# Casts of step 1's folds one step later where they stand at step 2 of a chunk

## The chip, the cores and the metric

The kernel runs on one core of a Trainium2 chip. The metric is the device time of one execution in microseconds (us); lower is better. Five engines of the core run side by side, each working through its own list of instructions in order: TensorE (PE in the profile, with its weight loads as PEld), VectorE (DVE), ScalarE (ACT), GpSimd (POOL) and SyncE (SP, which here only issues DMAs). They wait for each other by semaphores.

## The reference

The input `x` is 8 x 3136 x 256 in fp32. It goes through a two-dimensional Fourier transform of which the real part is kept, and then through one block of layer norm, two matrix products with a ReLU between them, and a residual sum:

```python
X = np.fft.fft(X, axis=1); X = np.fft.fft(X, axis=2); x = X.real
mu = np.mean(x, axis=-1, keepdims=True)
var = np.mean((x - mu) ** 2, axis=-1, keepdims=True)
xn = (x - mu) / np.sqrt(var + 1e-06) * g_ln
ch = np.maximum(xn @ w_ch1, 0.0) @ w_ch2          # 256 -> 1024 -> 256
return x + ch
```

## The kernel before

**Two halves that overlap.** The Fourier transform along the 3136 rows is done per batch b (0 to 7) in two steps with matmuls by tables (64 x 49). Step 1 works on 7 pieces of a batch; its results go to a scratch in memory and come back in another layout (`relayout`). Step 2 (line 309) turns them into columns of a *chunk*: 49 chunks of 256 tokens (the last is larger), each with its values (`ck`), their rounded part (`ckh`) and the rest (`ckl`). The norm and both products, here called the MoE part, run over the chunks. Products are made in three passes of rounded and rest operands (`hi`, `lo`), because one pass of the fast fp32r format is not exact enough.

**The main loop.** Line `for s in range(6, last)` counts steps; chunk c has the steps 8c to 8c+7, one per 128 of the 1024 inner columns. Below, "step 2 of its chunk" means s % 8 == 2. A step issues, in this order:

- `moe1_b(s-1)`: `h_hi` of the step before (ReLU and rounding, ACT, L368), and the rest `h_lo` (DVE, L369, which reads `h` and `h_hi`).
- `moe1_a(s)`: 6 matmuls into the PSUM tile `ab` (L354; two buffers, so the matmuls of step s need that the ones of step s-2 have been read), a copy of one half (`asb`, ACT, L359), and the sum and difference `h` (DVE, L360 and L361, which read `asb` and `ab`).
- what the table `late` holds for the step; `moe2(s-3)`: 12 matmuls (L404) of `h_hi`, `h_lo` with the second weights; and then what the table `after` holds for the step.

Nothing but these two tables, written out in the lines 606 to 669, and the order within a step set where an instruction stands on its engine. PE's list runs up to a step ahead of ACT's and DVE's.

**1/std.** For each chunk c the variance is ready in step 1 of the next chunk, where ACT takes the root (`std`, L460). In step 2 of that next chunk (`inverse_std` in `late` at 8c+10; for the chunks 0 and 1 one step later) four small DVE instructions on 128 x 2 values make 1/std: L467 (one input), then L468, L469 and L471, each with two inputs in SBUF. In the steps 3 and 4 `finish` (L477, L479) scales the product by it and adds the residual; these read PSUM and SBUF. `residual` (L428) is the last dimension's transform, at step 5, into the PSUM tiles that `finish` has freed.

**Step 1's folds.** For batches 1 to 7 a piece at step d (for batch 1 at d+1; list `steps1`) is prepared on POOL and ACT: `fold_zw` (two POOL sums, L207 and L208, listed at d-7), `fold_eo` (two POOL sums into `f`, L213 and L214, at d-6), `fold_hi` (the cast `fh` of `f`, ACT, L219, at d-4), `fold_lo` (the rest `fl`, POOL, L225, which reads `f` and `fh`, at d-3), and then `step1` (three matmuls, L262) and `store1`. All are in `after`, at the end of their step. `f`, `fh` and `fl` have two buffers each. POOL works in order and does little else, so it does `fl` of a piece as soon as ACT has cast it, and then goes straight on to the sums of the pieces that follow, long before the steps at which these are listed.

Before the change the 49 casts stand at the end of the steps 12, 15, 18, 21, 23, 26, 29 (batch 1), 34, 43, 44, 50, 58, 67, 74 (batch 2), and so on. 22 of them stand at step 2 of a chunk, 16 at step 3.

Of the kernel before, what the change touches and what calls it, by code (L numbers as in the profile page):

```python
# [146 lines left out]
def tile_kernel(ctx: ExitStack, tc: tile.TileContext, x, g_ln, w1, w2, tu, tab, tz, ty, tw, out):  # L147
# [460 lines left out]
    def add(s, fn, *args):  # L608

        after.setdefault(s, []).append((fn, args))  # L610
# [25 lines left out]
    for b in range(1, NB):  # L636
        need = 8 * (b * REG // CW) - 3
        at = steps1[b]
        ends_at = need - (58 if b > 1 else 30)
        add(need - 62 if b > 1 else ends_at - 7, ends, b)  # L640
        add(ends_at, step1_ends, b)
        for i, d in enumerate(at):
            d0, d = d, d - (b == 1)
            add(d - 7, fold_zw, b, i, nc.gpsimd)
            if b + 1 < NB:
                add(d - 5, load_x, b + 1, i)
            add(d - 6, fold_eo, b, i)
            add(d - 4, fold_hi, b, i)
            add(d - 3, fold_lo, b, i)
            add(d0, step1, b, i)  # L650
            add(d0, store1, b, i)
        add(at[-1] + 2, relayout, b)
# [201 lines left out]
```

## Time and profile before

| | |
|---|---|
| time, median of 3 runs | 1012.02 us (1011.04 to 1012.07) |
| the profiled execution | 1010.0 us, of which the span shown is 1008.2 us |
| granted TensorE clock in it | 0.999 |
| PE busy | 993.7 us, 99% of the span |
| DVE busy | 833.4 us, 83% |
| ACT busy | 534.6 us, 53% |
| POOL busy | 240.2 us, 24% |
| casts `fh` (ACT, L219) | 49 of 627 ns in the mean |
| rests `fl` (POOL, L225) | 49 of 1307 ns |
| 1/std, L468, L469, L471 (DVE) | 48 each of 394, 338 and 305 ns |

A row of a timeline has the start in us from the beginning of the span, the duration in us, the engine, line and operation, the tile written and the tiles read, shapes, and in brackets the idle time of the engine before the instruction with what ended it. A matmul's end is modelled: matmuls of 256 columns start 0.113 to 0.118 us apart and are shown 0.28 us long, so PE counts as busy in gaps of less than 0.16 us, and an idle time shown is that much too short. A row of the view by stretches has the stretch, its length, and for each engine the busy us and the number of instructions. A few matmul records are missing.

### The profile page before, as it was taken

To read this page: it belongs to the slowest core of one execution; us is meant where nothing else is said; L and a number is where in the kernel's file an instruction comes from. 1 tells how busy PE (TensorE), PEld (TensorE's weight loads), DVE (VectorE), ACT (ScalarE), POOL (GpSimd) and SP (SyncE) were. 2 spreads that over 40 slices of the span, in tenths; PEclk is the share of its full clock that TensorE was granted. 3 is DMA by queue.
4 is the path that set the end of the run, shared out by engine and by line. 5 is a ranking of instruction groups with operands and counts; after the bars stand their busy time and mean duration, and the time that the engine had idled before them with its cause. 6 is when DMAs were issued, how large, how long until landed. Compare 5 with 4: busy or idle time off the path is not lost.

```text
span 1008.2 us, 21760 instructions
## 1 busy us (share of the span) xinstructions
PE 993.7 (99%) x8289; PEld 969.7 (96%) x8289; DVE 833.4 (83%) x2190; ACT 534.6 (53%) x1416; POOL 240.2 (24%) x278
## 2 busy tenths in 40 slices
PE   9999999999999999999999999999999999999998
PEld 6799999999999999999999999999999999999998
DVE  6788887888888888887888887888888878887887
ACT  3655555554654555555555555554655555454553
POOL 1146433124212232312341125123322200000000
PEclk9999999999999999999999999999999999999999
DMA  9933352214221243121521242211311113100101
GB/s 344 262 145 125 107 161 81 79 58 136 86 93 54 75 141 100 55 74 62 170 74 64 84 129 93 90 58 64 116 43 43 53 43 96 43 23 22 43 22 43
DMA packets 41528, 92.10 MB, mean 91 GB/s; under 512 B 4176, under 2 KB 18704, under 8 KB 40528
## 3 DMA queue, kind: packets, MB, share of 16 engines
q1 hardware_dynamic: 40016, 88.87, 26.7%
q8 instruction: 66, 1.08, 0.5%
q0 software_dynamic: 320, 1.05, 0.3%
q10 hardware_dynamic: 1088, 0.79, 0.2%
q14 instruction: 38, 0.31, 0.1%
HBM read 50.32 MB, written 40.37 MB: 90 GB/s over the span
## 4 chain that ended last, share of the span: by engine, by line
PE 80%; DVE 13%; ACT 3%; DMA 2%; issue 2%; SPq 0%; ACTq 0%; DVEq 0%
PE acc L404 43%; PE ab L354 22%; PE ps L309 5%; DVE h_lo L369 4%; PE psy L428 4%; PE ps L262 3%; DVE h L361 2%; DVE h L360 2%; ACT h_hi L368 2%; DVE st L450 1%; DVE ve L468 1%; DVE ve L469 1%; DMA scratch<-s 1%; ACT s L265 1%; PE ps L255 1%
## 5 line engine op out<-in xcount | busy, mean ns | idle before, releaser
L404 PE MATMUL acc<-w_hi,h_lo 128*128 128x256 f32 x1568 | 435.7, 278 | 0.1
L404 PE MATMUL acc<-w_lo,h_hi 128*128 128x256 f32 x1568 | 435.5, 278 | 0.0
L404 PE MATMUL acc<-w_hi,h_hi 128*128 128x256 f32 x1568 | 435.5, 278 | 0.0
L368 ACT ACTIVATE h_hi<-h 128x512 fp32r<-128x512 f32 x392 | 249.7, 637 | 322.2 <-DVE h L361 322.1
L369 DVE SCALAR_TENSOR_TENSOR h_lo<-h,h_hi 128x512 fp32r<-128x512 f32 x392 | 287.5, 733 | 141.8 <-ACT h_hi L368 140.7
L404 PEld LDWEIGHTS acc<-w_hi,h_hi 128*128 128x128 f32 x1568 | 295.6, 189 | 0.0
L404 PEld LDWEIGHTS acc<-w_lo,h_hi 128*128 128x128 f32 x1568 | 295.1, 188 | 0.0
L404 PEld LDWEIGHTS acc<-w_hi,h_lo 128*128 128x128 f32 x1568 | 294.6, 188 | 0.4 <-DVE h_lo L369 0.3
L354 PE MATMUL ab<-ckl,w_hi 128*128 128x256 f32 x768 | 220.4, 287 | 6.5 <-DVE h L361 6.4
L354 PE MATMUL ab<-ckh,w_lo 128*128 128x256 f32 x768 | 213.9, 278 | 0.5 <-ACT ckh L330 0.4
L354 PE MATMUL ab<-ckh,w_hi 128*128 128x256 f32 x768 | 213.4, 278 | 0.0
L225 POOL TENSOR_TENSOR fl<-f,fh 128x512 fp32r<-128x512 f32 x49 | 64.1, 1307 | 527.1 <-ACT fh L219 478.4
L360 DVE TENSOR_TENSOR h<-asb,ab 128x256 f32<-128x256 f32 x384 | 158.3, 412 | 1.6 <-ACT asb L359 1.5
L361 DVE TENSOR_TENSOR h<-asb,ab 128x256 f32<-128x256 f32 x384 | 158.3, 412 | 0.0
L354 PEld LDWEIGHTS ab<-ckl,w_hi 128*128 128x128 f32 x768 | 144.3, 188 | 12.5 <-issue 7.6
L354 PEld LDWEIGHTS ab<-ckh,w_lo 128*128 128x128 f32 x768 | 144.7, 188 | 3.1 <-ACT ckh L330 0.5
L354 PEld LDWEIGHTS ab<-ckh,w_hi 128*128 128x128 f32 x768 | 144.8, 189 | 0.0
L359 ACT COPY asb<-ab 128x256 f32<-128x256 f32 x384 | 138.2, 360 | 10.8 <-PE ab L354 9.2
L265 ACT COPY s<-ps 128x508 f32<-128x508 f32 x56 | 32.8, 585 | 64.3 <-PE ps L262 50.5
L309 PE MATMUL ps<-tab_s,s 112*128 112x98 f32 (+1 forms) x512 | 65.5, 273 | 0.9 <-DMA s<-scratch 0.9
L309 PEld LDWEIGHTS ps<-tab_s,s 112*128 112x128 f32 x512 | 61.8, 191 | 1.4 <-PE pw L678 1.4
L330 ACT CAST ckh<-ps 128x392 fp32r<-128x392 f32 (+49 forms) x112 | 39.8, 356 | 29.5 <-PE ps L309 29.3
(108 smaller groups left out, 981.8 us busy)
## 6 DMA issues: line engine op xcount, KB each, us to landing
xs<-x SPq DMA_DIRECT2D x56, 512.0 KB, 4.1
out<-o SPq DMA_DIRECT2D x96, 256.0 KB, 2.0
scratch<-s SPq DMA_DIRECT2D x49, 256.0 KB, 2.3
s<-scratch SPq DMA_DIRECT2D x7, 1792.0 KB, 9.8
w1p_all<-w SPq DMA_DIRECT2D x8, 512.0 KB, 8.1
scratch<-s POOLq DMA_DIRECT2D x4, 256.0 KB, 6.1
s<-scratch SPq DMA_DIRECT2D x2, 448.0 KB, 5.6
s<-scratch SPq DMA_DIRECT2D x1, 896.0 KB, 12.0
```

The source lines that it names most:

```text
L225: nc.gpsimd.tensor_tensor(out=lo, in0=f, in1=hi.bitcast(F32), op=ALU.subtract)
L265: nc.scalar.copy(s[:, :, :, :127], ps[:, :, :, :127])
L309: nc.tensor.matmul(ps[:, h, k0 - base:k1 - base], s2[b][:KP, g, 128 * h:128 * h + 128], tab_s[:, h, k0:k1], start=(h == 0 and g == 2 * j), ...
L330: nc.scalar.copy(hi, src)
L354: nc.tensor.matmul(pt, wt[wi][:, j, fs], ch[xi][:, j, :w], start=(n == 0), stop=(n == 2))
L359: nc.scalar.copy(asb[:, :w], pa)
L360: nc.vector.tensor_tensor(out=h[:, :w], in0=asb[:, :w], in1=pb, op=ALU.add)
L361: nc.vector.tensor_tensor(out=h[:, w:], in0=asb[:, :m], in1=pb[:, :m], op=ALU.subtract)
L368: nc.scalar.activation(h_hi, h, AF.Relu)
L369: nc.vector.scalar_tensor_tensor(out=h_lo, in0=h, scalar=0.0, in1=h_hi.bitcast(F32), op0=ALU.max, op1=ALU.subtract)
L404: nc.tensor.matmul(acc[c, i][:, side], hs[xi][:, h0:h0 + 128], ws[wi][:, f], start=(f == 0 and side == 0 and n == 0), stop=(f == 7 and n = ...
L428: nc.tensor.matmul(ps[:, j, :129 + j], ck[:, j], ty_s[:, j, :129 + j], start=(j == 0), stop=True, skip_group_check=True)
```

## The change

Two lines of `tile_kernel` become three. `d` is the step that the piece's preparation is counted from. A piece with `d % 8 == 6` had its cast at d-4, which is step 2 of a chunk, and its rest at d-3; both go one step further back. All other pieces stay as they are.

```diff
         for i, d in enumerate(at):
             d0, d = d, d - (b == 1)
             add(d - 7, fold_zw, b, i, nc.gpsimd)
             if b + 1 < NB:
                 add(d - 5, load_x, b + 1, i)
             add(d - 6, fold_eo, b, i)
-            add(d - 4, fold_hi, b, i)
-            add(d - 3, fold_lo, b, i)
+            cast = (d - 4, d - 3)[d % 8 == 6]
+            add(cast, fold_hi, b, i)
+            add(cast + 1, fold_lo, b, i)
             add(d0, step1, b, i)
             add(d0, store1, b, i)
```

22 casts move from step 2 to step 3: those at 18, 26, 34, 50, 58, 74, 82, 106, 114, 130, 154, 162, 178, 194, 210, 218, 242, 258, 266, 290, 298 and 314. The lists of PE, DVE and SP keep their order. No instruction is added or removed.

**ACT, the steps 106 and 107** (batch 3, piece 4; in the names, the number of the step or of batch and piece comes first, the last number is the buffer's own). Before:

```order
L368 ACTIVATE h_hi105_4440<-h105_4422 128x512
L359 COPY asb106_4451<-ab106_4444 128x256
L219 CAST fh3_4_4473<-f3_4_4407 128x512
L368 ACTIVATE h_hi106_4475<-h106_4452 128x512
L359 COPY asb107_4486<-ab107_4479 128x256
L368 ACTIVATE h_hi107_4511<-h107_4487 128x512
```

With the change:

```order
L368 ACTIVATE h_hi105_4440<-h105_4422 128x512
L359 COPY asb106_4451<-ab106_4444 128x256
L368 ACTIVATE h_hi106_4473<-h106_4452 128x512
L359 COPY asb107_4484<-ab107_4477 128x256
L219 CAST fh3_4_4506<-f3_4_4407 128x512
L368 ACTIVATE h_hi107_4509<-h107_4485 128x512
```

The cast goes behind one `h_hi` and one copy of `ab`. In this piece, as in nearly all, POOL's list keeps its order: `fl` comes after the `f` of its own piece and before the sums of the next one.

**POOL, batch 1, pieces 5 and 6**, where the pieces follow each other at two or three steps. Before:

```order
L207 TENSOR_TENSOR zw1_6_1384<-xs_87 128x256
L208 TENSOR_TENSOR zw1_6_1384<-xs_87 128x256
L225 TENSOR_TENSOR fl1_5_1420<-f1_5_1310,fh1_5_1382 128x512
L213 TENSOR_TENSOR f1_6_1422<-zw1_6_1384 128x2x128
L214 TENSOR_TENSOR f1_6_1422<-zw1_6_1384 128x2x128
L225 TENSOR_TENSOR fl1_6_1549<-f1_6_1422,fh1_6_1505 128x512
```

With the change:

```order
L207 TENSOR_TENSOR zw1_6_1382<-xs_87 128x256
L208 TENSOR_TENSOR zw1_6_1382<-xs_87 128x256
L213 TENSOR_TENSOR f1_6_1420<-zw1_6_1382 128x2x128
L214 TENSOR_TENSOR f1_6_1420<-zw1_6_1382 128x2x128
L225 TENSOR_TENSOR fl1_5_1461<-f1_5_1310,fh1_5_1418 128x512
L225 TENSOR_TENSOR fl1_6_1549<-f1_6_1420,fh1_6_1505 128x512
```

The two sums of piece 6 now stand ahead of the rest of piece 5; the same happens with the sums of piece 3 and the rest of piece 2.

**ACT, the steps 34 to 36** (batch 2, piece 0), where the copies of `step1_ends` of batch 2 (L243, L245) stand at the end of step 35. Before:

```order
L265 COPY s1_1_912<-ps1_1_6_1700 128x4x127
L219 CAST fh2_0_1706<-f2_0_1634 128x512
L368 ACTIVATE h_hi34_1708<-h34_1679 128x512
L359 COPY asb35_1719<-ab35_1712 128x256
L243 COPY s1_2_1741<-pse0_2_1743 128x28
L245 COPY zmu_88<-pse0_2_1743 112x1
L368 ACTIVATE h_hi35_1752<-h35_1720 128x512
```

With the change:

```order
L265 COPY s1_1_912<-ps1_1_6_1700 128x4x127
L368 ACTIVATE h_hi34_1706<-h34_1679 128x512
L359 COPY asb35_1717<-ab35_1710 128x256
L243 COPY s1_2_1739<-pse0_2_1741 128x28
L245 COPY zmu_88<-pse0_2_1741 112x1
L219 CAST fh2_0_1747<-f2_0_1634 128x512
L368 ACTIVATE h_hi35_1750<-h35_1718 128x512
```

The cast now stands behind these two copies and right in front of `h_hi` of step 35.

## The prediction

> **What bounds the kernel now.** I read the page's busy times and the chain first:
>
> ```profile
> PE 993.7 (99%) x8289; PEld 969.7 (96%) x8289; DVE 833.4 (83%) x2190; ACT 534.6 (53%) x1416; POOL 240.2 (24%) x278
> PE 80%; DVE 13%; ACT 3%; DMA 2%; issue 2%; SPq 0%; ACTq 0%; DVEq 0%
> ```
>
> PE sets the time: its list is full, and a change that adds no matmul can win only what PE waits, or how fast it issues. The chain's 13% on DVE say that it does wait for DVE. The view of waits, for PE alone and from 100 to 820 us (where the casts of step 1 stand), has one row:
>
> ```profile
> PE ab L354 <- DVE h L361: 4.9, 9, 0.7
> ```
>
> Nine waits, all of the same kind: the first matmul into an `ab` buffer waits until DVE has read that buffer. So I looked in the timeline at what DVE did before one of them. Here the cast stands at the end of step 58, a piece that the change moves:
>
> ```profile
> 186.36 0.62 ACT L219 CAST fh<-f 128x512 fp32r<-128x512 f32 x1
> 187.06 1.30 POOL L225 TENSOR_TENSOR fl<-f,fh 128x512 fp32r<-128x512 f32 x1 [15.32 <-ACT fh L219]
> 187.18 0.41 DVE L361 TENSOR_TENSOR h<-asb,ab 128x256 f32<-128x256 f32 x1
> 187.62 0.63 ACT L368 ACTIVATE h_hi<-h 128x512 fp32r<-128x512 f32 x1 [0.64 <-DVE h L361]
> 187.70 0.67 DVE L468 SCALAR_TENSOR_TENSOR ve<-ve 128x2 f32<-128x2 f32 x1
> 188.31 0.73 POOL L207 TENSOR_TENSOR zw<-xs 128x256 f32<-128x256 f32 x1
> 188.41 0.65 DVE L469 TENSOR_TENSOR ve<-ve 128x2 f32<-128x2 f32 x1
> 189.00 0.64 POOL L208 TENSOR_TENSOR zw<-xs 128x256 f32<-128x256 f32 x1
> 189.09 0.56 DVE L471 SCALAR_TENSOR_TENSOR r<-ve 128x2 f32<-128x2 f32 x1
> 189.58 0.68 DVE L369 SCALAR_TENSOR_TENSOR h_lo<-h,h_hi 128x512 fp32r<-128x512 f32 x1
> 190.51 0.41 DVE L361 TENSOR_TENSOR h<-asb,ab 128x256 f32<-128x256 f32 x1
> ...
> 190.13 0.28 PE L404 MATMUL acc<-w_hi,h_hi 128*128 128x256 f32 x1
> 191.06 0.36 PE L354 MATMUL ab<-ckl,w_hi 128*128 128x256 f32 x1 [0.65 <-DVE h L361]
> ...
> 197.17 0.39 PE L262 MATMUL ps<-fl,t_hi 128*128 128x512 f32 x1
> ```
>
> Each of the three small DVE operations ends just after a POOL operation does: L468 at 188.37 (`fl` at 188.36), L469 at 189.06 (`zw` at 189.04), L471 at 189.65 (the second `zw` at 189.64). They stand still until POOL has finished. The sum L361 at 187.18, which reads one tile in SBUF and one in PSUM, does not: it is as long beside `fl` as at 190.51. Now a piece that the change does not touch, with its cast at the end of step 99, which is step 3 of its chunk:
>
> ```profile
> 285.03 0.16 DVE L467 RECIPROCAL ve<-ve 128x2 f32<-128x2 f32 x1
> 285.61 0.16 DVE L471 SCALAR_TENSOR_TENSOR r<-ve 128x2 f32<-128x2 f32 x1
> 285.94 0.62 ACT L219 CAST fh<-f 128x512 fp32r<-128x512 f32 x1
> 286.64 1.30 POOL L225 TENSOR_TENSOR fl<-f,fh 128x512 fp32r<-128x512 f32 x1 [12.40 <-ACT fh L219]
> 287.87 0.68 DVE L369 SCALAR_TENSOR_TENSOR h_lo<-h,h_hi 128x512 fp32r<-128x512 f32 x1
> 287.89 1.25 POOL L207 TENSOR_TENSOR zw<-xs 128x256 f32<-128x256 f32 x1
> ```
>
> 1/std is over before `fl` begins: all four operations take 0.74 us (285.03 to 285.77), where L468 to L471 alone took 1.95 above (187.70 to 189.65). `fl` ends as the next `h_lo` starts, and it is the `zw` behind it that now waits for DVE (1.25 in place of 0.73). DVE operations with two SBUF inputs and POOL's exclude each other. This is also a rule of the Trainium skill ("SBUF — State Buffer", section "Who interferes with whom"): such an instruction and a GpSimd one that reads SBUF exclude each other for a whole instruction, whoever comes first. By that rule the trace's rows agree (0.67 beside 0.16).
>
> So the nine waits come from casts at step 2: `fl` and what follows it on POOL fall on 1/std, DVE is 1.4 us late (0.67 + 0.65 + 0.56 in place of 3 x 0.16), and PE, two steps of `ab` on, has to wait.
>
> **The change, part by part.** Nothing is added or removed; 22 casts (0.62 us of ACT) and rests (1.30 of POOL) begin one step, about 2.1 us, later. I compare whole chunks, from one chunk's first `residual` matmul to the next's, since a wait's price has parts that the 4.9 us lack (a matmul is shown 0.28 long but the next one starts 0.113 later). Stretches, with length, then busy us and instructions per engine:
>
> ```profile
> 174.25:194.13 19.88, 19.23 (x166) 18.92 (x165) 16.67 (x44) 10.21 (x27) 4.40 (x5) 1.00 0.20 68
> ...
> sum 196.64, PE 192.44 PEld 189.65 DVE 163.72 ACT 102.90 POOL 46.38; mean PE 19.24 PEld 18.97 DVE 16.37 ACT 10.29 POOL 4.64
> ...
> 213.92:232.90 18.98, 18.98 (x165) 18.84 (x164) 15.69 (x42) 10.25 (x28) 5.57 (x8) 1.00 0.16 57
> 824.64:843.54 18.90, 18.90 (x165) 18.76 (x164) 15.43 (x45) 9.69 (x26) 0.00 (x0) 1.00 0.48 140
> ...
> sum 79.13, PE 79.13 PEld 77.78 DVE 65.29 ACT 42.87 POOL 25.09; mean PE 19.78 PEld 19.44 DVE 16.32 ACT 10.72 POOL 6.27
> 271.83:292.32 20.49, 20.49 (x176) 20.23 (x175) 16.82 (x45) 11.35 (x31) 7.31 (x9) 1.00 0.26 91
> 331.83:351.62 19.79, 19.79 (x173) 19.65 (x172) 16.48 (x46) 10.90 (x29) 4.78 (x7) 1.00 0.23 81
> 450.38:470.66 20.28, 20.28 (x173) 20.15 (x172) 16.46 (x46) 10.90 (x29) 5.32 (x7) 1.00 0.23 79
> 587.79:608.71 20.92, 20.92 (x179) 20.79 (x179) 17.94 (x47) 11.23 (x33) 4.99 (x6) 1.00 0.52 164
> 706.57:727.02 20.45, 20.45 (x179) 20.31 (x178) 17.33 (x46) 11.13 (x31) 4.84 (x5) 1.00 0.46 142
> ...
> 109.95 0.36 PE L354 MATMUL ab<-ckl,w_hi 128*128 128x256 f32 x1 [0.66 <-DVE h L361]
> ```
>
> 1. *Ten chunks with a cast at step 2, one step 1 and one group of step 2* (the first row and, over all ten, the first sum): 196.64 us. The same PE work undisturbed takes 18.90 where step 1 stands at step 6, and 18.98 where it stands at step 7; six and four of the ten are such: 6 x 18.90 + 4 x 18.98 = 189.32. **Gain 7.3.**
> 2. *Four chunks with two step 1 and a cast at step 2* (the sum 79.13). A chunk with two step 1, a second group of step 2 and no cast at step 2 takes 20.49; the second group is worth 19.79 - 18.90 = 0.89; 4 x 19.60 = 78.40. **Gain 0.7.**
> 3. *Two chunks behind such waits that run slower without a wait of their own.* 450.38 takes 20.28 for the work of 19.79, 587.79 takes 20.92 for that of 20.45. PE is busy in the whole of them, with as many instructions (173, 179): it is the pace at which it issues that differs. Each comes right behind one of the ten chunks above, so the wait there may leave the pace behind; but so do 331.83 and 706.57, which are quick. Bounds 0 and 1.0; I take the upper part, since no slow stretch quoted comes behind an undisturbed one: **gain 0.7**.
> 4. *Piece 5 of batch 1 (26 to 27).* The wait at 109.95 costs what that at 191.06 does: (191.06 - 190.13 - 0.11) + 0.08 for the longer first matmul = **gain 0.9**. That the sums of piece 6 now go first on POOL costs nothing: POOL sits idle before each rest (15.32 us at 187.06).
> 5. *Piece 2 of batch 1 (18 to 19).* 1/std of chunk 1 stands one step later than the others', so here the rest moves onto it, not away. But POOL's sums fall on it already:
>
> ```profile
> 85.16 0.55 DVE L468 SCALAR_TENSOR_TENSOR ve<-ve 128x2 f32<-128x2 f32 x1
> ```
>
>    Whether it stands still for sums or for a rest is the same: **0**; bounds: one rest, 1.30, either way.
> 6. *Piece 0 of batch 2 (34 to 35).* Here the cast goes behind the copies of `step1_ends`, and the first of them waits 3.12 us:
>
> ```profile
> 127.50 1.35 DVE L369 SCALAR_TENSOR_TENSOR h_lo<-h,h_hi 128x512 fp32r<-128x512 f32 x1 [0.38 <-ACT h_hi L368]
> 130.86 0.21 ACT L243 COPY s<-pse 128x28 f32<-128x28 f32 x1 [3.12 <-issue]
> 130.99 0.65 ACT L368 ACTIVATE h_hi<-h 128x512 fp32r<-128x512 f32 x1
> 133.76 0.47 DVE L479 SCALAR_TENSOR_TENSOR o<-acc,r,y 128x256 f32<-128x256 f32 x1
> ...
> PEld psy L428 <- DVE o L479: 0.3, 1, 0.3
> ```
>
> The cast then stands between the copies and `h_hi` at 130.99, which comes 0.5 us later, and the rest begins as `h_lo` does, which can add up to 0.67 (1.35 against 0.68). `finish` at 133.76 is late already: PE's `residual` waits 0.3 for it (last row, from the waits of 126 to 136 us), and whatever is added shows on PE. Bounds: 1.2 (both), and 0 (the 1.35 at 127.50 become 0.68, and what is late here was late already). **Loss 1.0**, near the upper one, since the 3.12 us end with ACT's copies and what follows these sets `h_lo`.
>
> Elsewhere the later cast delays nothing that PE sees: the rest at 187.06 ends at 188.36; a step later, an eighth of 19 us, that is 190.7, and its matmul starts at 197.17. `h_hi` of step 3 waits behind the cast by 0.5 us at most, as it does at 285.94 without a wait of PE. SP's list is unchanged, and what it loads next for a piece hangs on sums that stand long before.
>
> Sum: 7.3 + 0.7 + 0.7 + 0.9 - 1.0 = 8.6. The profiled execution took 1010.0 us in all, 2.0 under the median shown; 1010.0 - 8.6 = 1001.4, and 1012.02 - 8.6 = **1003.4**.
>
> **The rivals.**
>
> - *Half of it comes back.* Behind the rest come four POOL sums that fall on `h_lo` of step 4 and 5 instead of on 1/std; the row at 287.89 shows POOL waiting, and a few `h_lo` will wait 0.5 us. If in half of the chunks PE waits for that, 4.3 remain: 1007.7. For it: after chunks with a wait removed, PE is further ahead of DVE than now. Against it: 16 casts at step 3 stand there today, and the nine waits hold none of theirs.
> - *Slower: the rest blocks `h_lo`, which is in every step, in place of 1/std.* Place: step 4, from the point where `fl` ends after `h_hi` of step 3 is ready. Today it ends at 287.94 when `h_lo` starts at 287.87, so there is nothing to spare. If every moved rest missed it as at 127.50 (0.67) and PE had no slack, 21 x 0.67 = 14 us (one of the 22 pays it today): 1003 + 14 = 1017. By the Trainium skill's rule above, too, a rest that comes first holds `h_lo`; 127.50 bears that out. Against it: a rest follows its cast, and the cast the copy of `ab`, in the same order as at 285.94. It needs ACT to lag in most chunks.
> - *The wait is the cast's, not the rest's.* If ACT's 0.62 us in front of `h_hi` made DVE late, the same waits would come one step later: 1012. For it: the nine all follow a cast. Against it: at 189.58 `h_lo` starts when L471 ends; `h_hi` (187.62) had been ready for over a microsecond.
>
> **How the numbers follow.** Chances: the forecast 0.79; half of it 0.11; no change 0.06; slower 0.04. A measurement tells this kernel from no change from about 0.2%, 2 us. Half of the gain still counts as faster, so faster is 0.90, no change 0.06, slower 0.04. The range reaches down to all gains at their upper bounds with nothing lost at step 35 (7.3 + 0.7 + 1.0 + 0.9 = 9.9) and the lowest of the runs shown, 1.0 below the median: 1012.0 - 9.9 - 1.0 = 1001; and up to half of it, 1007.7, called 1008. What is left out is the two last cases and some of the edges.
>
> **What will show it.** Right: the row of nine waits is gone or down to one or two; L468, L469 and L471 average under 0.2 us (now 394, 338 and 305 ns), with chunk 1's as the exception; the first ten stretches take 18.9 to 19.0; DVE's busy time falls by some 20 us. Wrong: waits of `ab` for DVE at steps 5 to 6; `h_lo` rows of 1.3 us at step 4; slow-pace chunks as many as before; a wait at step 37 of over 1.5 us would make part 6 too small.

## The result and the profile after

| | before | with the change |
|---|---|---|
| time, median of 4 runs each, on one chip | 1011.53 us (1010.36 to 1012.07) | 1001.40 us (1000.91 to 1001.50) |
| ratio, 95% interval | | 0.990 (0.9883 to 0.9918) |
| the profiled execution | 1010.0 us | 1001.5 us |
| its span | 1008.2 us | 999.7 us |

The change makes the kernel 1.0% faster, 10.1 us by the medians and 8.5 us from one profiled execution to the other; 1003.4 us were predicted, from a sum of 8.6 us. The difference between 10.1 and 8.5 is not the change's: the profiled execution of before (1010.0) was quicker than each of its four runs, that of the changed kernel (1001.5) was not.

The page of the changed kernel, busy times, the shares of the chain, and the group of the `h_lo` operations (count, busy us, mean ns of one, idle time ahead of them and what ended most of it):

```profile
PE 988.3 (99%) x8288; PEld 966.4 (97%) x8289; DVE 817.8 (82%) x2190; ACT 534.8 (53%) x1416; POOL 248.3 (25%) x278
PE 88%; DVE 7%; ACT 2%; DMA 1%; issue 1%; ACTq 0%; SPq 0%; DVEq 0%
L369 DVE SCALAR_TENSOR_TENSOR h_lo<-h,h_hi 128x512 fp32r<-128x512 f32 x392 | 295.5, 754 | 148.7 <-ACT h_hi L368 146.6
```

DVE's share of the chain has gone from 13% to 7%, and its busy time from 833.4 to 817.8 us with the same 2190 instructions. Nothing was taken off DVE; its instructions stand still less. In the view of waits, PE alone and 100 to 820 us, the row of nine waits of 4.9 us is gone, and one other row stands there:

```profile
PE psy L428 <- DVE o L479: 1.0, 1, 1.0
```

The three small operations of 1/std, in the view by lines (busy us, mean ns of one), now take what they take alone, but for those of chunk 1:

```profile
L468 DVE SCALAR_TENSOR_TENSOR ve<-ve 128x2 f32<-128x2 f32 (+1 forms) x49 | 8.4, 171 | 1.7
L469 DVE TENSOR_TENSOR ve<-ve 128x2 f32<-128x2 f32 (+1 forms) x49 | 8.4, 171 | 1.7
L471 DVE SCALAR_TENSOR_TENSOR r<-ve 128x2 f32<-128x2 f32 (+1 forms) x49 | 8.3, 169 | 1.7
```

The timeline at the piece that the prediction showed, whose cast has gone from step 58 to 59:

```profile
188.26 0.16 DVE L468 SCALAR_TENSOR_TENSOR ve<-ve 128x2 f32<-128x2 f32 x1
...
188.66 0.16 DVE L471 SCALAR_TENSOR_TENSOR r<-ve 128x2 f32<-128x2 f32 x1
188.85 0.69 DVE L369 SCALAR_TENSOR_TENSOR h_lo<-h,h_hi 128x512 fp32r<-128x512 f32 x1
188.98 0.62 ACT L219 CAST fh<-f 128x512 fp32r<-128x512 f32 x1
189.68 1.29 POOL L225 TENSOR_TENSOR fl<-f,fh 128x512 fp32r<-128x512 f32 x1 [14.59 <-ACT fh L219]
190.81 0.28 PE L354 MATMUL ab<-ckl,w_hi 128*128 128x256 f32 x1
190.91 0.69 DVE L369 SCALAR_TENSOR_TENSOR h_lo<-h,h_hi 128x512 fp32r<-128x512 f32 x1
190.94 1.25 POOL L207 TENSOR_TENSOR zw<-xs 128x256 f32<-128x256 f32 x1
192.97 1.17 DVE L369 SCALAR_TENSOR_TENSOR h_lo<-h,h_hi 128x512 fp32r<-128x512 f32 x1
```

1/std is over at 188.82 and `fl` begins at 189.68. The first sum `zw` now stands still for `h_lo` (1.25 in place of 0.73), and an `h_lo` one step later for a sum (1.17 in place of 0.69). The matmul at 190.81 has no wait.

The same stretches as in the prediction (chunk by chunk, by PE's first `residual`): the first of the ten, the sums over the ten and over the four, the two that ran at a slow pace, and the two in which batch 1's piece 5 and step 35 lie. Columns: stretch, length, then busy us and instructions of PE, PEld, DVE, ACT and POOL, then the granted clock.

```profile
174.82:193.72 18.90, 18.90 (x166) 18.76 (x164) 15.04 (x43) 10.20 (x27) 4.23 (x6) 1.00 0.19 60
sum 189.32, PE 189.32 PEld 187.94 DVE 154.45 ACT 103.09 POOL 44.33; mean PE 18.93 PEld 18.79 DVE 15.45 ACT 10.31 POOL 4.43
sum 78.39, PE 78.39 PEld 77.36 DVE 64.47 ACT 42.84 POOL 26.42; mean PE 19.60 PEld 19.34 DVE 16.12 ACT 10.71 POOL 6.60
446.46:466.25 19.79, 19.79 (x173) 19.65 (x172) 16.67 (x46) 10.94 (x29) 5.79 (x8) 1.00 0.24 81
582.28:602.72 20.44, 20.44 (x179) 20.30 (x178) 17.13 (x46) 11.11 (x31) 6.35 (x7) 1.00 0.55 167
90.34:112.92 22.58, 21.24 (x172) 20.30 (x170) 19.50 (x49) 13.65 (x35) 10.71 (x11) 1.00 0.41 137
133.48:155.22 21.74, 20.76 (x175) 20.44 (x174) 18.99 (x51) 12.26 (x33) 10.90 (x13) 1.00 0.50 159
```

Set against the same chunks before (196.64, 79.13, 20.28, 20.92, and 23.12 and 20.97 in the rows below), they have changed by -7.32, -0.74, -0.49, -0.48, -0.54 and +0.77 us: -8.80. One more chunk with a moved cast (the one from 232.90 before) is 0.25 shorter, the first 90 us are 0.51 longer, and all other chunks are as long as before within 0.01 us. That is the span's 8.5.

```profile
89.83:112.95 23.12, 21.17 (x171) 20.10 (x170) 20.05 (x47) 13.58 (x35) 10.66 (x11) 1.00 0.37 122
133.51:154.48 20.97, 20.83 (x175) 20.50 (x175) 17.76 (x48) 12.17 (x33) 6.13 (x7) 1.00 0.51 164
```

### The profile page after: what moved, and what is told of

It reads as the page before. It is cut to its first block, busy times and chain, and to the rows that moved or that the text cites. A ratio compares the mean times of both kernels' runs of the same rounds, so it can differ in the third digit from the quotient of the medians.

```text
span 999.7 us, 21759 instructions
## 1 busy us (share of the span) xinstructions
PE 988.3 (99%) x8288; PEld 966.4 (97%) x8289; DVE 817.8 (82%) x2190; ACT 534.8 (53%) x1416; POOL 248.3 (25%) x278
## 4 chain that ended last, share of the span: by engine, by line
PE 88%; DVE 7%; ACT 2%; DMA 1%; issue 1%; ACTq 0%; SPq 0%; DVEq 0%
PE acc L404 49%; PE ab L354 24%; PE ps L309 5%; PE psy L428 4%; PE ps L262 3%; DVE h_lo L369 2%; DVE h L360 1%; DVE h L361 1%; ACT h_hi L368 1%; PE pw L679 1%; PE ps L255 1%; DMA scratch<-s 1%; PE ps L257 1%; DMA s<-scratch 1%; DVE st L450 0%
## 5 line engine op out<-in xcount | busy, mean ns | idle before, releaser
L369 DVE SCALAR_TENSOR_TENSOR h_lo<-h,h_hi 128x512 fp32r<-128x512 f32 x392 | 295.5, 754 | 148.7 <-ACT h_hi L368 146.6
```

The source lines that it names most:

```text
L369: nc.vector.scalar_tensor_tensor(out=h_lo, in0=h, scalar=0.0, in1=h_hi.bitcast(F32), op0=ALU.max, op1=ALU.subtract)
```

## The experiments

The theory: PE waited because POOL's rest, and the sums that it works through behind the rest, fell on the three small operations of 1/std, which then stand still until POOL's instruction ends. Against it: the cast on ACT in front of `h_hi` is the cause; the rest alone is; or the later place comes at a price of its own.

e1 to e4 ran on one chip, on which the kernel before took 1009.81 us; e5, e6, e7 and e9 on another (1010.58 us); e10 on a third (1008.42 us). The times expected start from the 1001.4 us of the chip on which the kernel before took 1011.53. So a time 1 to 3 us under an expected range says little, and the stretches and the ratios decide. From 150 to 820 us the chunks of e1 are as long as those of the changed kernel within 0.01 us, so e1 stands for the change in comparisons on its chip.

**e1: the cast also at its old place.** The changed kernel, with a second, useless cast of the 22 pieces at step 2. It writes the same tile; only ACT does more.

```diff
+            if d % 8 == 6:
+                add(d - 4, fold_hi, b, i)
             add(cast, fold_hi, b, i)
```

> The changed kernel, and each of the 22 moved pieces is cast once more at its old place, the end of step 2 of the chunk (the same tile is written twice; the rest on POOL still follows the second cast). So ACT has its 0.62 us back at the old place and POOL has nothing there. Theory (POOL's rest and sums make 1/std stand still): no waits of ab for DVE after 150 us, L468, L469 and L471 near 0.16 us in these chunks, 1001.4 to 1002.5 us. Rival (the cast itself in front of h_hi makes DVE late): the nine waits are back, one step 2 after the other, 1009 to 1012 us.

Measured: 1000.79 us, ratio 0.9917 (0.9902 to 0.9931). The page has the 22 casts on ACT, 11.4 us of them:

```profile
PE 988.7 (99%) x8289; PEld 966.8 (97%) x8289; DVE 817.3 (82%) x2190; ACT 546.2 (55%) x1438; POOL 247.0 (25%) x278
```

No wait of PE is listed between 150 and 820 us, and the chunks there are as long as with the change alone. So the cast at step 2 costs nothing there, and the rival that blames it falls.

**e2: the rest also at its old place.** The cast and the rest are done at the old places and again at the new ones. Since the sums stand behind the second rest, the first stands alone beside 1/std.

```diff
+            if d % 8 == 6:
+                add(d - 4, fold_hi, b, i)
+                add(d - 3, fold_lo, b, i, False)
             add(cast, fold_hi, b, i)
             add(cast + 1, fold_lo, b, i)
```

> As the run with two casts, but POOL also makes the rest at the old place, and again after the second cast; the sums of the next piece come only after the second rest. So of what fell on 1/std in the kernel before, the rest alone is back (1.30 us of POOL), without the sums behind it. Theory: L468 stands still for about 0.5 us (mean near 390 ns again), L469 and L471 do not (under 200 ns); DVE is late by 0.5 in place of 1.4 us, and as waits of 0.55 to 0.81 were left of 1.4, nothing or nearly nothing reaches PE: 1001.4 to 1003.5 us. If the rest alone is the whole cause: 1009 to 1011. Rival (the cast): 1009 to 1012 us, whatever L468 does.

Measured: 1002.48 us, ratio 0.9932 (0.9917 to 0.9947). Again no wait of PE from 150 to 820 us. The small operations, by lines (L472, L473 and L475 here):

```profile
L472 DVE SCALAR_TENSOR_TENSOR ve<-ve 128x2 f32<-128x2 f32 (+1 forms) x49 | 19.1, 389 | 1.7
L473 DVE TENSOR_TENSOR ve<-ve 128x2 f32<-128x2 f32 (+1 forms) x49 | 9.5, 193 | 1.7
L475 DVE SCALAR_TENSOR_TENSOR r<-ve 128x2 f32<-128x2 f32 (+1 forms) x49 | 8.9, 181 | 1.7
```

The first one stands still as it did before the change (389 ns), the other two hardly (193 and 181, from 334 and 303). One held operation makes DVE 0.5 us late, and PE has no listed wait for it. It is not free, though: from 150 to 820 us the chunks of e2 are together 1.8 us longer than e1's, 1.5 of it in three chunks of 0.49 each, which come behind a chunk with one held operation and in which PE issues at a slower pace. The first of them, 19.79 us with the change:

```profile
192.34:212.62 20.28, 20.28 (x173) 20.15 (x172) 17.52 (x46) 10.99 (x30) 5.49 (x6) 1.00 0.21 79
```

So with the first operation alone held, 1.8 us are left of the 9.3 by which these chunks were longer before the change. The greater part, and the waits, come with three held operations in a row, one per POOL instruction: the rest *and* the two sums that follow it. That the rest alone is the whole cause falls too. Three held operations are not always enough: in the kernel before, the chunks from 351.62 and 470.66 have all three (1.88 us in all for L468, L469 and L471), and they take 19.63 and 19.64 us, as they do with the change.

**e3: 1/std one step earlier, casts where they were.** The kernel before, with only this:

```diff
-        add_late(8 * c + 10 + (c < 2), inverse_std, c)
+        add_late(8 * c + 9 + (c < 2), inverse_std, c)
```

> The kernel before, with its casts and rests where they were, but with the four DVE operations of 1/std one step earlier (step 1 of a chunk in place of step 2; one later for the chunks 0 and 1 as before). Theory: it is the meeting of 1/std and POOL's rest that costs, so this does as well as moving the casts: no waits of ab after 150 us, L468 to L471 near 0.16 us, 1000.5 to 1002.5 us (the loss at step 37 of batch 2's piece 0 doesn't arise). Rival (casts or rests at step 2 delay h_lo or ACT by themselves): 1009 to 1012 us, the waits stay.

Measured: 997.91 us (996.28 to 998.99), ratio 0.9886 (0.9871 to 0.9901). No wait of PE from 150 to 820 us; the three operations take 173, 171 and 171 ns. The same waits go without a cast being moved, so it is the meeting of the two that costs, whichever side moves. The time is below the range expected: it also beats the change, by 2.9 us against e1 on the same chip (1000.79 us, 999.78 to 1002.11). In the stretches of the profiled executions, 0.8 us comes from leaving step 35 alone (20.97 us in place of 21.74) and 1.7 from batch 1 (20.92 in place of 22.58), where the change gained 0.54:

```profile
89.82:110.74 20.92, 20.78 (x171) 20.22 (x170) 17.74 (x45) 12.37 (x32) 11.11 (x11) 1.00 0.37 128
```

**e4: 16 other casts put onto 1/std.** The changed kernel, with the 16 casts that stand at step 3 put to step 2:

```diff
-            cast = (d - 4, d - 3)[d % 8 == 6]
+            cast = d - 3 if d % 8 == 6 else d - 5 if d % 8 == 7 else d - 4
```

> The changed kernel, and in addition the 16 pieces that had their cast at step 3 all along (d % 8 is 7) get it at step 2: the cost that was taken away, put where it never was. Theory: each of these chunks follows a chunk with one group of step 2, as the ten that waited did; waits of 0.5 to 0.9 us in most of the 16 and some slow stretches behind them: 1009 to 1017 us. Rival (the place is harmful only in the chunks where it was): 1001 to 1003 us.

Measured: 1007.19 us (1004.68 to 1009.46), ratio 0.9975 (0.9966 to 0.9985). Slower than e1 on the same chip by 6.4 us, but less than expected. The waits of PE from 150 to 820 us:

```profile
PE ab L354 <- DVE h L361: 2.6, 4, 0.7
```

Four of the sixteen give a wait. These four chunks take 82.95 us in all; without one such a chunk takes 19.79 (79.16). Here is the first of them, and behind it a piece that gives none:

```profile
207.94 0.67 DVE L468 SCALAR_TENSOR_TENSOR ve<-ve 128x2 f32<-128x2 f32 x1
208.55 0.73 POOL L207 TENSOR_TENSOR zw<-xs 128x256 f32<-128x256 f32 x1
208.65 0.65 DVE L469 TENSOR_TENSOR ve<-ve 128x2 f32<-128x2 f32 x1
209.34 0.56 DVE L471 SCALAR_TENSOR_TENSOR r<-ve 128x2 f32<-128x2 f32 x1
211.31 0.36 PE L354 MATMUL ab<-ckl,w_hi 128*128 128x256 f32 x1 [0.66 <-DVE h L361]
...
266.55 1.29 POOL L225 TENSOR_TENSOR fl<-f,fh 128x512 fp32r<-128x512 f32 x1 [8.74 <-PE ab L354]
267.18 0.68 DVE L468 SCALAR_TENSOR_TENSOR ve<-ve 128x2 f32<-128x2 f32 x1
267.89 0.16 DVE L469 TENSOR_TENSOR ve<-ve 128x2 f32<-128x2 f32 x1
```

In eight of the sixteen pieces sums follow the rest and three operations are held (0.67 + 0.65 + 0.56); four of these eight give the wait, here of 0.66. In the other eight no such sums follow, little more than the first operation is held, and none gives a listed wait. This is e2's finding in the other direction, and where the expectation went wrong: it counted every rest beside 1/std as a wait. But the listed waits are only half of the price. From 150 to 820 us the chunks are 7.2 us longer than with the change; the four with a wait make 3.8 of it, and 3.4 lie in fifteen others, 0.03 to 0.33 us each, in which no wait is listed. Why four chunks with three held operations have room for them was not worked out.

**e5: step 35 undone.** The changed kernel, with the cast of piece 0 of batch 2 back at step 34:

```diff
-            cast = (d - 4, d - 3)[d % 8 == 6]
+            cast = (d - 4, d - 3)[d % 8 == 6 and (b, i) != (2, 0)]
```

> The changed kernel with one part undone: piece 0 of batch 2 keeps its cast at step 34. Theory (the later cast stands behind a copy that waits for a DMA, and its rest meets h_lo): the wait of residual for finish goes from 1.0 back to about 0.3 us, and the stretch from the residual of step 37's chunk before it (some 20.97 before, 21.74 with the change) is 20.97 again; 0.8 us faster than the changed kernel, 1000.0 to 1001.0 beside 1001.4 us. If the loss there is a DMA's chance, the stretch stays near 21.7 us.

Measured: 999.43 us, ratio 0.9888 (0.9872 to 0.9905). The wait of `residual` (window 55 to 150 us) and the stretch:

```profile
PE psy L428 <- DVE o L479: 0.2, 1, 0.2
...
133.05:153.94 20.89, 20.76 (x175) 20.44 (x174) 17.76 (x48) 12.12 (x33) 6.12 (x7) 1.00 0.54 167
```

1.0 of wait becomes 0.2, and 21.74 us become 20.89: at this place the later cast costs the change 0.85 us. In the whole time that is less than the scatter of the runs; the stretch shows it. But it takes a late copy as well. In e2 the cast stands at the same place (and once more at step 34). There the copy L243 came after a wait of 0.99 us, for PE, where it waited 3.54 with the change, and the stretch took 20.02 us. Why the copy was released earlier in that run stays open.

**e6: two steps later.** The changed kernel with the 22 casts at step 4:

```diff
-            cast = (d - 4, d - 3)[d % 8 == 6]
+            cast = (d - 4, d - 2)[d % 8 == 6]
```

> The changed kernel, with the 22 casts at step 4 in place of step 3 (two steps later than before). Theory: any place after 1/std will do as long as rest and sums find gaps; the sums now fall on step 5 and 6, where PE has some 1.8 us more work: 1000.5 to 1003 us, no waits after 150 us. Rival (step 3 is the one good place, since at step 5 ACT's copies of a chunk stand behind the cast): waits at step 6 or 7, 1003 to 1010 us.

Measured: 997.46 us (997.10 to 998.61), ratio 0.9873 (0.9858 to 0.9888). It was expected above 1000 and did better. PE does not wait from 150 to 820 us, as with the change; the gain is in the two stretches where the change was poor:

```profile
89.03:110.28 21.25, 21.05 (x171) 20.32 (x170) 17.59 (x43) 12.28 (x32) 11.39 (x13) 1.00 0.37 127
130.84:150.86 20.02, 20.02 (x176) 19.88 (x174) 17.20 (x47) 11.61 (x33) 11.32 (x13) 1.00 0.54 169
```

In the second one the cast comes a step after the two copies and no longer between them and `h_hi`. From 150 to 820 us the chunks are as long as with the change within 0.01 us: a later cast has no price there, at step 3 or at step 4.

**e7: the three operations with one SBUF tensor each.** The kernel before, with L468, L469 and L471 written as six operations on one column, whose other factor is a value per partition:

```diff
-        eng.scalar_tensor_tensor(out=a, in0=q, scalar=-0.5, in1=q, op0=ALU.mult, op1=ALU.mult)
-        eng.tensor_tensor(out=a, in0=a, in1=v, op=ALU.mult)
...
+                eng.tensor_scalar(out=ak, in0=qk, scalar1=qk, scalar2=-0.5, op0=ALU.mult, op1=ALU.mult)
+                eng.tensor_scalar(out=ak, in0=ak, scalar1=vk, scalar2=1.5, op0=ALU.mult, op1=ALU.add)
+                eng.tensor_scalar(out=r[:, k:k + 1], in0=ak, scalar1=qk, scalar2=None, op0=ALU.mult)
```

> The kernel before, casts and rests where they were, but L468, L469 and L471 are written as operations with one tile read and the second value as a per-partition scalar, one column at a time (6 of 128x1 in place of 3 of 128x2; the last chunk as before). Theory, as the rule of two inputs has it: these don't exclude POOL, they are 0.16 us each beside the rest, 1/std takes 1.1 us in every chunk, DVE is later by 0.4 us everywhere and by 1.1 us less where it was held; no or few waits, 1001 to 1004 us. Rival (a scalar read from SBUF excludes POOL as well, or any small operation does): six that stand still, up to 3 us, 1011 to 1025 us.

Measured: 1008.65 us (1007.17 to 1009.38), ratio 0.9979 (0.9970 to 0.9988): hardly a gain, and a miss. The timeline beside the rest of the piece cast at step 58:

```profile
186.11 1.29 POOL L225 TENSOR_TENSOR fl<-f,fh 128x512 fp32r<-128x512 f32 x1 [15.08 <-ACT fh L219]
186.74 0.21 DVE L472 TENSOR_SCALAR ve<-ve 128x1 f32<-128x1 f32 x1
186.99 0.21 DVE L473 TENSOR_SCALAR ve<-ve 128x1 f32<-128x1 f32 x1
...
187.35 0.73 POOL L207 TENSOR_TENSOR zw<-xs 128x256 f32<-128x256 f32 x1
187.86 0.21 DVE L474 TENSOR_SCALAR r<-ve 128x1 f32<-128x1 f32 x1
```

The mechanism holds: four of the six operations start while `fl` runs (until 187.40) and two beside the sum behind it, and none is held; of the 288 in the whole run none takes more than 0.22 us. But one takes 0.21 us, and 1/std as a whole 1.5 (186.55 to 188.07), where it took 0.74 undisturbed; and it takes that in every chunk, not in 22. That makes DVE later by an estimated 0.7 to 0.8 us in each (1.5 less 0.74). Waits come up (from 150 to 820 us two are listed, of 0.6 us each in the mean), and many chunks are 0.3 to 0.5 us longer than with the change, such as 19.19 and 19.39 in place of 18.90. The hold was traded for a price in many chunks.

**e9: e3, and the copies of `step1_ends` a step later.** In addition to e3, `step1_ends` of batch 2 goes from step 35 to 36:

```diff
-        ends_at = need - (58 if b > 1 else 30)
+        ends_at = need - (30 if b == 1 else 57 if b == 2 else 58)
```

> The run with 1/std one step earlier, and the matmuls and copies of step1_ends of batch 2 one step later (36 for 35), so that the copy L243 need not wait for the store of batch 1's last piece. Theory: its wait of 3.1 us on ACT is gone, the stretch of 20.97 us there becomes 20.0 to 20.3, 0.7 to 1.0 us faster than the run with 1/std earlier alone: 996.5 to 997.5 us beside 997.9. Rival: the wait was hidden and nothing moves, 997.9 us.

Measured: 997.82 us (996.91 to 998.84), ratio 0.9875 (0.9860 to 0.9890). The stretch falls from e3's 20.97 to

```profile
133.21:153.22 20.01, 20.01 (x175) 19.87 (x174) 16.30 (x46) 11.42 (x31) 6.01 (x6) 1.00 0.55 173
```

So, with the cast at step 34, 0.96 us of it had hung on the copies' wait. The whole time can't be told from e3's: the first 90 us were 1.9 us longer in this execution (that chunk starts at 91.73, not 89.82).

**e10: all three.** e6, e3 and e9 in one kernel: casts at step 4, 1/std one step earlier, the copies at step 36.

> All that gained by itself, together: the 22 casts at step 4, 1/std one step earlier, step1_ends of batch 2 at step 36. Theory: each removes the same meetings of 1/std and POOL, so they don't add up; after 150 us nothing is left to gain, and in batch 1 (70 to 135 us) 20.9 us or a little less is left of the stretch that took 23.1: 996.5 to 997.8 us, no faster than the best of the three by more than 1 us. Rival (POOL's work at two different places helps twice): under 996 us.

Measured: 997.56 us (997.15 to 998.83), ratio 0.9897 (0.9880 to 0.9913), with before at 1008.42 us on that chip. Nothing is added: each of the edits takes away meetings that the others take away too, and what is gone can't be won twice. In batch 1 the stretch takes 21.49 us, more than the 20.9 expected and than e3's 20.92. The best versions are e6, e3, e9 and e10, 997.5 to 997.9 us, some 3 us under the change (e1, which has the change's list on PE, took 1000.79 on the chip on which e3 took 997.91). Among themselves they can't be told apart.

## Why the prediction was right

- **What bounds.** Right. PE's list did not change, and what was won is what PE had waited for DVE, with the pace behind it. The waits came from the three small operations; e1 and e3 show it from both sides. That these stand still because they read two tiles in SBUF is borne out by e7: written with one tile and a value per partition, they are not held beside the same rest and sums.
- **The account was too coarse in one point.** "`fl` and what follows it on POOL fall on 1/std" took both together. e2 and e4 show that they differ: the rest alone holds one operation, 0.5 us, which gives no listed wait and costs 1.8 us over all chunks from 150 to 820 us; it is the two sums behind it that bring DVE's delay to 1.4 us and most of the loss.
- **Parts 1 and 2** (7.3 and 0.7): 7.32 and 0.74. To price whole chunks by undisturbed ones was worth it. Eight of the nine waits lie in eight of the ten chunks, with 4.2 us, and these eight lost 6.6. The other two (568.67 and 687.18) have no wait and only the first operation held; they lost 0.7 behind a chunk with a wait.
- **Part 3** (0.7, bounds 0 and 1.0): 0.97. Both slow chunks are quick now, 19.79 and 20.44. The reading that a wait in the chunk ahead leaves the slow pace does not hold as it stands. The chunk ahead of the second one (568.67) has no wait, and in e2 three chunks run slowly without a listed wait anywhere. What all of these have ahead of them is a held operation of 1/std, and that is not enough, since other chunks behind one stayed quick. So the size was near, and the mechanism of this term is open.
- **Part 4** (0.9): 0.54. The mis-sized term: the wait at 109.95 was priced at its full length and nothing was put down for what replaces it. That wait is gone, but PE starts its matmul at 107.03 0.35 us after the one ahead, where the pace there is 0.118, and the last 18 matmuls ahead of step 2 now come at the slower pace. In the stretch 1.34 us aren't covered by busy PE (22.58 - 21.24). Most of that is one wait, which was there before as well (1.21, at 96.57). It is not listed in e3 and e6, where the stretch takes 20.92 and 21.25. Which late operation of DVE brings it was not taken apart.

```profile
97.05 0.47 PE L262 MATMUL ps<-fl,t_hi 128*128 128x512 f32 x1 [1.20 <-DVE ckl L334]
```

- **Part 5** (0): 1/std of chunk 1, all four operations, took 2.03 us before and 2.14 now, as thought, though the first two stretches together are 0.36 us longer. How much of that is the change can't be said: e3 and e9, whose edits do not differ in the first 90 us, differ there by 1.9 us.
- **Part 6** (loss 1.0, bounds 0 and 1.2): 0.77 in the stretch, and 0.85 by e5, with the copy late; without that (e2) the loss did not come. The rows are those that were named: the copy's wait, the cast behind it, `h_hi` after the cast, a held `h_lo` of 1.35, a late `finish`:

```profile
130.91 0.21 ACT L243 COPY s<-pse 128x28 f32<-128x28 f32 x1 [3.54 <-issue]
131.04 0.64 ACT L219 CAST fh<-f 128x512 fp32r<-128x512 f32 x1
131.56 0.65 ACT L368 ACTIVATE h_hi<-h 128x512 fp32r<-128x512 f32 x1
132.24 1.35 DVE L369 SCALAR_TENSOR_TENSOR h_lo<-h,h_hi 128x512 fp32r<-128x512 f32 x1 [2.96 <-ACT h_hi L368]
134.57 0.47 DVE L479 SCALAR_TENSOR_TENSOR o<-acc,r,y 128x256 f32<-128x256 f32 x1
```

- **Not counted.** Five chunks with a moved cast were in no group. The one from 232.90 became 0.25 us shorter; those from 213.92, 351.62, 470.66 and 805.66 stayed as they were. The prediction took the first of these four, 18.98 us, for an undisturbed one; the price was right all the same, since it is 18.98 with the change too.
- **DVE's busy time** fell by 15.6 us, not by some 20. 1/std gave back 25 us, as the three lines show (19.1 + 16.4 + 14.8 before, 8.4 + 8.4 + 8.3 now), but `h_lo` took 8.0 more, 733 to 754 ns in the mean. So the rival "half of it comes back" had its mechanism right: POOL's sums now hold `h_lo`. What it had wrong is the price. `h_lo` is one operation, held once, by half a microsecond (1.17 at 192.97), and the chunks with the change (18.90 and 18.98) show no loss from it.
- **The slower rival** did not come: in the piece above `fl` begins (189.68) after `h_lo` of its step has (188.85), and PE has no wait of that kind from 155 us on. At step 35, where the copies had made ACT late, it happened as described.
- **The total.** 1003.4 was the sum taken from the median shown then, 1012.02; taken from the profiled execution it gave 1001.4, and 1001.5 was measured there. The 2.0 us between them are scatter of the kernel before: by the medians the change gained 10.1, and the 1001.40 us lie at the lower end of the range. That the sum of 8.6 meets the 8.5 between the profiled executions so closely is in part luck: the parts are off by 0.0 to 0.4 us each way, the first 90 us lost 0.5 that no part had, and 232.90 gained 0.25.

## What to carry to other kernels

Where DVE has a chain of tiny operations with two SBUF inputs, keep POOL's instructions off it: each POOL instruction holds one operation until it ends, so three operations of 0.16 us took 1.9, while one large operation (`h_lo`) was held once, by half a microsecond. Look at what the delayed engine is late by: from 150 us on 0.5 us late cost at most 0.1 us in most chunks and 0.5 us in three (e2), while 1.4 us late cost 0.65 to 0.98 us in each of eight, and nothing in two others. And price a wait by whole stretches against undisturbed ones of the same work: the idle time listed for those eight chunks was 4.2 us of the 6.6 that they lost, and chunks with no listed wait lost time too.

## What the runs showed of the hardware

PE issues the same 256-column matmuls at one of two paces at a granted clock of 1.00. In one chunk of the changed kernel, ahead of the `step1` (L262, at 449.50) and some 12 us behind it:

```profile
448.67 0.28 PE L404 MATMUL acc<-w_hi,h_hi 128*128 128x256 f32 x1
...
449.38 0.28 PE L404 MATMUL acc<-w_hi,h_hi 128*128 128x256 f32 x1
...
462.45 0.28 PE L354 MATMUL ab<-ckl,w_hi 128*128 128x256 f32 x1
...
463.13 0.28 PE L404 MATMUL acc<-w_hi,h_lo 128*128 128x256 f32 x1
```

From 448.67 to 449.38 six matmuls start 0.118 us apart; from 462.45 to 463.13 six start 0.113 apart. In the kernel before, the same chunk (from 450.38) has the two paces the other way round: 0.113 us from 452.01 to 453.25, ahead of its `step1`, and 0.118 behind it to the end, and takes 20.28 us in place of 19.79. In e2 the pace goes from 0.113 to some 0.118 at 189.34, without a wait, and the next chunk is the one of 20.28 us shown above. So the pace changes at a `step1` in these chunks, and in e2 at a place where no wait is listed. What sets it was not found.

The other point is that the time of a small operation depends on its form: 0.16 us for two tensors of 128 x 2, 0.21 for one column with a value per partition (e7), though the second handles half as many elements.
